# Storing the result of a decode kernel by four transfers on two queues instead of one on one queue

## The chip, the cores and the metric

The kernel runs on one core of a Trainium2 chip. The time is that of the device, in microseconds, for one execution of the program; beside it stands a profile of one such execution. A core has TensorE (PE; its weight loads are listed as PEld), VectorE (DVE), ScalarE (ACT), GpSimd (POOL) and SyncE (SP), and sixteen DMA engines that move data between HBM and the on-chip memory. In the profile a `q` behind an engine's name means its sequencer: the part that waits, branches and issues DMA transfers. L631 is line 631 of the kernel.

## The reference

Two blocks work on the same input x of 2 rows by 1024, and a gate mixes them. Block A is one decode step of attention with 32 query heads over 4 key and value heads and a cache of 32768 positions; block B is a mixer with a small MLP.

```
g = sigmoid((x * gate_w).sum(-1, keepdims=True))
q = (x @ wq), 32 heads of 128
p = softmax(q @ k.T * 128 ** -0.5)          # k_cache, v_cache: 2 x 4 x 32768 x 128
a = (p @ v) @ wo
h = gelu(layernorm(x) @ w1)                 # shifted along the sequence, which has length 1
x1 = x + shifted(h) @ w2
b = x1 + gelu(layernorm(x1) @ w3) @ w4
out = g * a + (1 - g) * b                   # 2 x 1 x 1024, float32
```

With a sequence of length 1 every shift moves h out of reach, so x1 is x, and w1 and w2 aren't read. What has to be read are the two caches and wq, w3, w4 and wo, 331 MB in float32; what is written are 8 KB.

## The kernel before

Everything is ordered by hand. Each engine has its own instruction stream, and a small class `Line` holds an engine and its semaphore: `after` makes the engine wait for marks of others, `mark` lets an instruction raise the engine's own semaphore, and `take` (L52) waits for a semaphore with a no-op and lowers it again.

All large loads are issued by SyncE through the helper `load` (L218), in the order of use, into two ring buffers `load0` and `load1` of 8 MB each: wq and w3 for the projections, then for each of eight pairs of batch row and key head two pieces of the keys (kt) and two of the values (vt), with w4 after the fourth pair, then wo. The end of wo goes into a buffer of its own, `tail`, by four transfers. The first two loads are issued ahead of everything (L246), and ScalarE issues one small load, that of x and the gate's weights (L279). Every load waits until TensorE has read what stood in its buffer.

TensorE, VectorE and ScalarE follow the loads in loops over the eight pairs. ScalarE's last work is its part of the copies in the eighth pair (L547). After the loop, TensorE multiplies the last rows of wo (`into_acc`, L372; `into_final`, L380), with the sum so far folded in by a product with a selection matrix (L617). VectorE copies one half of the final sums into `ahead` (L627) and adds the other half into `out_sb` (L630).

The result is laid out in 128 partitions of 64 numbers, of which every fourth partition holds a row that counts: 32 rows of 256 bytes. Partition 32g + 4r holds columns 64g to 64g + 63 of row r of `out`, which has 8 rows of 256 columns. One transfer stores them, issued by SyncE (L631). Behind it SyncE raises `issued` (L632), GpSimd waits for that and clears all semaphores but `stored` (L634), and ScalarE's `take` waits until the store has landed. That `take` is the last thing that the kernel does.

```
    dve.after(ended(2))
    sp.after(dve.mark(nc.vector.tensor_add(out_sb, final[1], ahead)))
    nc.sync.dma_start(out.rearrange("(q b) (g c) -> g (q b) c", q=G, g=G), out_sb[::SHIFT // B]).then_inc(stored, 16)
    nc.sync.nop().then_inc(issued, 1)
    nc.gpsimd.wait_ge(issued, 1)
    nc.clear_and_free_semaphores(cleared)
    act.take(stored, 16)
```

Here G is 4, CHUNK 64, SHIFT 8, B 2 and C 32.

Of the kernel before, what the change touches and what calls it, by code (L numbers as in the profile page):

```python
# [15 lines left out]
B, D, HQ, HKV, SK, DH, F = 2, 1024, 32, 4, 32768, 128, 3584  # L16
# [7 lines left out]
C = 32  # L24
G = P // C
# [3 lines left out]
SHIFT = C // G  # L29
CHUNK = D // G // G  # L30
# [42 lines left out]
def kernel(  # L73
# [52 lines left out]
    nc = tc.nc  # L126
    scale = DH ** -0.5

    def new(name, *shape, parts=P):
        return nc.alloc_sbuf_tensor(name, [parts, *shape], F32).ap()  # L130
# [51 lines left out]
    ahead = new("ahead", CHUNK)  # L182
    out_sb = new("out_sb", CHUNK)
# [5 lines left out]
    final = [sc[i][:, :CHUNK] for i in range(2)]  # L189
# [6 lines left out]
    def sem(name):  # L196
        cleared.append(nc.alloc_semaphore(name))
        return cleared[-1]

    stored = nc.alloc_semaphore("stored")  # L200
    pe, dve, act, pool = (Line(e, sem(n)) for e, n in (
        (nc.tensor, "pe"), (nc.vector, "dve"), (nc.scalar, "act"), (nc.gpsimd, "pool")))
    sp = Line(nc.sync)
# [4 lines left out]
    issued = sem("issued")  # L208
# [32 lines left out]
    def ended(i):  # L241
        return (pe.sem, SUMMED[1] + i)
# [32 lines left out]
    for mark, lo, hi in zip(came[1:], (0, 5, 7), (5, 7, 8)):  # L275
# [7 lines left out]
        out=ident, in_=ident, pattern=[[-1, P]], base=0, channel_multiplier=1,  # L283
# [343 lines left out]
    nc.vector.tensor_copy(ahead, final[0]).then_inc(own_step, 1)  # L627
    dve.take(own_step)
    dve.after(ended(2))
    sp.after(dve.mark(nc.vector.tensor_add(out_sb, final[1], ahead)))  # L630
    nc.sync.dma_start(out.rearrange("(q b) (g c) -> g (q b) c", q=G, g=G), out_sb[::SHIFT // B]).then_inc(stored, 16)  # L631
    nc.sync.nop().then_inc(issued, 1)  # L632
    nc.gpsimd.wait_ge(issued, 1)
    nc.clear_and_free_semaphores(cleared)  # L634
    act.take(stored, 16)


# ---- launch: one core; the host only lays the arrays out
# [28 lines left out]
```

## Time and profile before

| | |
|---|---|
| median of 3 runs | 773.53 us (773.42 to 773.77) |
| the profiled execution | 773.49 us |
| its span, first to last instruction | 772.0 us |
| read from HBM, written | 331.36 MB, 0.01 MB |
| mean rate over the span | 429 GB/s |
| TensorE, VectorE, ScalarE busy | 57%, 12%, 8% |

The span counts from the first instruction of any engine to the last; the time of the execution has 1.5 us more, which no row of the profile covers. Times in the views are in microseconds from the span's start, except durations in the rows by line, which are in nanoseconds (smallest, median and largest). A DMA row on a sequencer is the issue of a transfer, not its movement of data; that shows only in the share of the DMA engines, which the views by windows give for any stretch.

### The profile page before, as it was taken

The numbers are of one execution on the slowest core, as the hardware profiler recorded it, in microseconds if no ns is written. First come the engines' busy times: TensorE is split into PE (matmuls) and PEld (weight loads), VectorE is DVE, ScalarE is ACT, GpSimd is POOL, SyncE is SP. The second block draws the span as 40 slices with busy tenths as digits, with TensorE's granted clock in tenths as the row PEclk, the third lists the DMA queues.
The fourth block names the chain that finished last, engine by engine and source line by source line (L and its number), as shares of the span: only waits on it lengthen the run. The fifth ranks groups of instructions, "written<-read, shape, count | busy, mean of one in ns | idle before, by whom it ended". The sixth has DMA issues, their size and how long they took to land. (4 is left out here: it accounts for less than half of the span.)

```text
span 772.0 us, 7477 instructions
## 1 busy us (share of the span) xinstructions
PE 439.1 (57%) x3348; PEld 202.4 (26%) x3348; DVE 95.0 (12%) x274; ACT 60.4 (8%) x143; POOL 3.9 (1%) x14
## 2 busy tenths in 40 slices
PE   0676756464645474556475447454746564646466
PEld 0232413222322232223233213121323232313233
DVE  1110102100210021002100002100210021002110
ACT  0000002000200020002000002000200020002000
POOL 2000000000000000000000000000000000000000
PEclk9977668867787768767866677777776697678789
DMA  9999999999999999999999999999999999999997
GB/s 381 435 436 436 435 436 435 436 436 431 421 435 435 435 435 435 435 435 435 430 428 444 432 435 435 435 431 435 435 435 435 435 435 435 435 435 431 421 430 321
DMA packets 6668, 331.50 MB, mean 429 GB/s; under 512 B 900, under 2 KB 1028, under 8 KB 1284
## 3 DMA queue, kind: packets, MB, share of 16 engines
q1 hardware_dynamic: 6516, 331.36, 99.3%
q8 instruction: 7, 0.11, 0.1%
q10 hardware_dynamic: 144, 0.01, 0.0%
q14 instruction: 1, 0.01, 0.0%
HBM read 331.36 MB, written 0.01 MB: 429 GB/s over the span
## 5 line engine op out<-in xcount | busy, mean ns | idle before, releaser
L474 PE MATMUL sc<-load,q_cur 128*32 128x512 f32 x1024 | 149.4, 744 | 126.3 <-PEq L52 126.3
L500 PE MATMUL pv<-load,pt 128*32 128x512 f32 x1024 | 131.0, 670 | 92.5 <-PEq L52 92.5
L474 PEld LDWEIGHTS sc<-load,q_cur 128*32 128x32 f32 x1024 | 54.2, 133 | 215.4 <-issue 209.5
L500 PEld LDWEIGHTS pv<-load,pt 128*32 128x32 f32 x1024 | 39.4, 121 | 174.1 <-issue 174.1
L491 PE MATMUL sc<-wide,p 128*128 128x128 f32 x256 | 43.8, 344 | 22.8 <-PEq L52 22.8
L557 DVE TENSOR_REDUCE mx<-sc 128x1 f32<-128x512 f32 x32 | 21.4, 689 | 284.3 <-PE sc L474 284.3
L541 ACT ACT_TABLE_LOAD x8 | 10.3, 1283 | 490.5 <-ACTq L52 490.5
L491 PEld LDWEIGHTS sc<-wide,p 128*128 128x128 f32 x256 | 39.5, 182 | 30.0 <-issue 30.0
L372 PE MATMUL acc<-load,w_pad 128*32 128x256 f32 x448 | 33.9, 474 | 18.5 <-PEq L52 18.5
L574 DVE COPY pt<-sc 64x256 f32<-64x256 f32 x64 | 25.9, 415 | 73.4 <-PE sc L491 72.8
L547 ACT COPY pt<-sc 64x256 f32<-64x256 f32 x64 | 23.5, 368 | 77.4 <-PE sc L491 75.3
L579 DVE COPY pv_sb<-pv 128x512 f32<-128x512 f32 x16 | 10.3, 686 | 153.4 <-PE tr L506 153.4
L372 PEld LDWEIGHTS acc<-load,w_pad 128*32 128x32 f32 x448 | 18.6, 136 | 33.0 <-issue 28.2
L510 PE MATMUL tr<-sel,pv_sb 128*128 128x8 f32 x128 | 19.3, 287 | 11.8 <-PEq L52 11.8
L358 PE MATMUL sc<-load,x_pad 128*32 128x512 f32 x128 | 19.9, 790 | 3.8 <-PEq L52 3.8
L510 PEld LDWEIGHTS tr<-sel,pv_sb 128*128 128x128 f32 x128 | 18.8, 233 | 12.3 <-issue 12.3
L541 ACT ACTIVATE p<-sc,bias 128x512 f32<-128x512 f32 x32 | 21.6, 686 | 0.1
L358 PE MATMUL sc<-load,xn_pad 128*32 128x384 f32 (+1 forms) x128 | 16.0, 662 | 7.6 <-PEq L52 7.6
L343 PE MATMUL tr<-xg_sb,perm 128*128 128x16 f32 x4 | 1.0, 372 | 25.2 <-DMA xg_sb<-xg 25.2
L570 DVE COPY p<-p 128x256 f32<-128x256 f32 x32 | 9.4, 294 | 26.7 <-ACT p L541 26.7
L358 PEld LDWEIGHTS sc<-load,xn_pad 128*32 128x32 f32 x128 | 4.9, 133 | 18.7 <-issue 18.7
L358 PEld LDWEIGHTS sc<-load,x_pad 128*32 128x32 f32 x128 | 5.0, 138 | 17.8 <-issue 17.8
(93 smaller groups left out, 95.0 us busy)
## 6 DMA issues: line engine op xcount, KB each, us to landing
load<-w SPq DMA_DIRECT2D x4, 7168.0 KB, 24.5
load<-wo SPq DMA_DIRECT2D x1, 7168.0 KB, 29.0
load<-wo SPq DMA_DIRECT2D x1, 4608.0 KB, 18.9
load<-wo SPq DMA_DIRECT2D x1, 2560.0 KB, 24.7
tail<-wo SPq DMA_DIRECT2D x1, 1024.0 KB, 26.7
tail<-wo SPq DMA_DIRECT2D x1, 640.0 KB, 27.7
load<-kt SPq DMA_DIRECT2D x16, 29.7
load<-vt SPq DMA_DIRECT2D x16, 29.1
```

What stands on the lines that cost most here:

```text
L358: last = nc.tensor.matmul(b[C * g:C * g + C, :hi - lo], pad[:, k], t[:, o + lo:o + hi], start=(k == 0), stop=(k == KD - 1))
L372: inst = nc.tensor.matmul(acc[C * g:C * g + C], lhsT, rows[:, g * (D // G):(g + 1) * (D // G)], start=False, stop=last, skip_group_check=True)
L474: last = nc.tensor.matmul(sc[i][C * g:C * g + C], q_cur[:, w, s], ring[j][:, w, o:o + 512], start=(s == 0 and w == 0), stop=(s == 1 and w ...
L491: last = nc.tensor.transpose(sc[k][:, t * P:(t + 1) * P], pair.rearrange("p w q -> p (w q)"), ident)
L500: last = nc.tensor.matmul(pv[C * g:C * g + C], pt[j][w][:, lo:lo + C], ring[j][:, w, o:o + G * DH], start=(j == 0 and w == 0 and t == 0), ...
L510: last = nc.tensor.matmul(tr[1][:, w * REP:(w + 1) * REP], pv_sb[:, s, w].rearrange("p i q -> p (i q)"), sel[:, s], start=(s == 0), stop=( ...
L541: nc.scalar.activation(p[:, i, :, :PART], sc[i].rearrange("p (t q w) -> p t w q", t=NT, w=PART), AF.Exp, bias=bias, scale=scale, accum_out ...
L547: nc.scalar.copy(*halves(1, j, c)).then_inc(pt_in, 1)
L557: last = [nc.vector.reduce_max(out=mx[:, k:k + 1], in_=sc[k], axis=AX.X) for k in ((1, 2) if i == 2 else (i,))][-1]
L570: nc.vector.tensor_copy(p[:, i, :, PART], p[:, i, :, 0]).then_inc(to_pe, 1)
L574: nc.vector.tensor_copy(*halves(0, j, c)).then_inc(pt_in, 1)
L579: last = nc.vector.tensor_copy(pv_sb[:, :, :, i], pv.rearrange("p (s q w) -> p s w q", q=HALF, w=PART))
```

## The change

The transfer with three dimensions (four blocks of columns, eight rows, 64 numbers) becomes four transfers with two dimensions, one for each block of columns. SyncE issues the first and the third, ScalarE the second and the fourth. Both engines wait for the same addition, both raise `issued` when they are done, GpSimd waits for two instead of one, and ScalarE's `take` waits for the landing of all four.

```
-    sp.after(dve.mark(nc.vector.tensor_add(out_sb, final[1], ahead)))
-    nc.sync.dma_start(out.rearrange("(q b) (g c) -> g (q b) c", q=G, g=G), out_sb[::SHIFT // B]).then_inc(stored, 16)
-    nc.sync.nop().then_inc(issued, 1)
-    nc.gpsimd.wait_ge(issued, 1)
+    added = dve.mark(nc.vector.tensor_add(out_sb, final[1], ahead))
+    for line in (sp, act):
+        line.after(added)
+    for g in range(G):
+        line = (sp, act)[g % 2]
+        line.e.dma_start(out[:, g * CHUNK:(g + 1) * CHUNK], out_sb[C * g:C * g + C:SHIFT // B]).then_inc(stored, 16)
+    for line in (sp, act):
+        line.e.nop().then_inc(issued, 1)
+    nc.gpsimd.wait_ge(issued, 2)
     nc.clear_and_free_semaphores(cleared)
-    act.take(stored, 16)
+    act.take(stored, 16 * G)
```

## The prediction

> **What bounds the kernel now.** I read the page's head and its DMA lines first, to see what the 772 us are spent on.
>
> ```profile
> span 772.0 us, 7477 instructions
> ...
> DMA  9999999999999999999999999999999999999997
> ...
> q1 hardware_dynamic: 6516, 331.36, 99.3%
> ```
>
> The sixteen DMA engines are full from the first slice to the last but one, so the kernel as a whole is a stream of weights and caches from HBM. The change touches none of that: it edits the store of the result, which is issued once the stream has ended. A stage of two microseconds is in question, and the limit of that stage is a chain, not a bandwidth. So the second view is the chain that ended last, from its last piece of the stream on.
>
> ```profile
> 740.75 27.75 DMA tail<-wo
> 768.49 0.04 issue
> 768.53 0.77 PE sc L380 x40
> 769.30 0.11 PE sc L617 x8
> 769.41 0.46 PE sc L380 x24
> 769.87 0.02 issue
> 769.89 0.23 DVE out_sb L630
> ```
>
> The last load lands at 768.49, TensorE and VectorE finish the last products, and the addition into out_sb ends at 769.89 + 0.23 = 770.12. The chain view stops at this instruction of an engine, though the span goes on to 772.0. What follows stands in the rows by line: the issue on SyncE (L631), the mark behind it (L632), GpSimd's clearing of semaphores (L634), and the one instruction of ScalarE that waits for the store (L52, the helper `take`).
>
> ```profile
> SPq L631 <- DVE out_sb L630: 28.0, 1, 28.0
> ...
> L631 SPq DMA_DIRECT2D out<-out_sb x1: 672/672/672, 770.1 to 770.1; - x1
> ...
> L632 SPq EVENT_SEMAPHORE  x1: 17/17/17, 770.9 to 770.9; - x1
> ...
> L634 POOLq DRAIN  x1: 82/82/82, 770.9 to 770.9; - x1
> L634 POOLq EVENT_SEMAPHORE_RANGE_CLEAR  x1: 135/135/135, 771.0 to 771.0; - x1
> ...
> L52 ACTq EVENT_SEMAPHORE  x1: 17/17/17, 771.9 to 771.9; - x1
> ```
>
> The third view is the busy time by windows, cut where the DMA engines begin and end their work for the store.
>
> ```profile
> 770.15:770.82 0.67, 0.00 (x0) 0.00 (x0) 0.00 (x0) 0.00 (x0) 0.00 (x0) 1.00 0.00 0
> 770.82:771.42 0.60, 0.00 (x0) 0.00 (x0) 0.00 (x0) 0.00 (x0) 0.00 (x0) 1.00 0.00 0
> 771.42:771.60 0.18, 0.00 (x0) 0.00 (x0) 0.00 (x0) 0.00 (x0) 0.00 (x0) 0.94 0.20 44
> 771.60:771.96 0.36, 0.00 (x0) 0.00 (x0) 0.00 (x0) 0.00 (x0) 0.00 (x0) 0.50 0.00 0
> ```
>
> The second last number of a row is the mean share of the sixteen DMA engines, the last one GB/s. So the tail reads: 0.03 from the addition to the issue, 0.67 of issue, 0.60 in which the issue is over and no packet runs, 0.18 of packets, and 0.35 until ScalarE's `take` at about 771.95, just ahead of the end of the span. Together 1.83 us, 0.24% of the run. Nothing covers any of it: no engine is busy in these rows. The measured execution is 773.49, that is 1.5 beyond the span; that part lies behind ScalarE's last instruction and I let it move with it.
>
> **The change part by part.** It removes one issue of 0.67 on SyncE. It adds two issues on SyncE and two on ScalarE, each of 8 rows of 256 bytes, a wait of ScalarE for the addition, a second mark, and a count of two for GpSimd. The bytes stay the same (32 rows, 8 KB). Only the terms 0.67 and 0.18 can change in kind; the 0.60 and the 0.35 are latencies that the last of four transfers pays as the one transfer did, so I keep them at the rows.
>
> The price of an issue with two dimensions is not in the trace for a store, but it is for loads:
>
> ```profile
> L218 SPq DMA_DIRECT2D load<-kt x16: 327/328/328, 70.0 to 663.2; - x16
> ...
> L218 SPq DMA_DIRECT2D tail<-wo x4: 432/432/432, 740.3 to 741.7; - x4
> ...
> L246 SPq DMA_DIRECT2D load<-wq x2: 387/400/412, 0.7 to 1.2; - x2
> ...
> L279 ACTq DMA_DIRECT2D xg_sb<-xg x1: 372/372/372, 2.4 to 2.4; - x1
> ...
> 740.27 1.85 SPq L218 DMA_DIRECT2D tail<-wo  x4
> ```
>
> The issues of kt come alone, behind a wait, and take 0.328. The four of tail come right behind another issue and take 0.432 each; four of them fill 1.85, so the three gaps are (1.85 − 4 × 0.432) / 3 = 0.04. ScalarE's only issue, of xg, took 0.372. So two issues on one queue at the loads' price take 0.328 + 0.04 + 0.432 = 0.80, and on ScalarE 0.372 + 0.04 + 0.432 = 0.84. That is already more than the single 0.67: even if the third dimension was the whole reason for the dearer store, what is bought back on the first issue is spent on the second. The other bound is the store's own row: 0.672 + 0.04 + 0.672 = 1.38 for two, and 1.49 if the second also pays the 0.104 by which 0.432 exceeds 0.328. The new transfers share the two dimensions with the loads, and the direction, the short rows and the few partitions with the store. I take the side of the loads, since dimensions are what an issuing sequencer has to work through, but only two thirds of the way: 0.80 + (1.38 − 0.80) / 3 = 0.99. The last issue then ends 0.99 − 0.67 = 0.32 later than now. The bounds are +0.13 and +0.82; a bound below nothing needs an issue cheaper than any in the trace, and stands as a rival.
>
> Both queues start together, since ScalarE waits for the same mark as SyncE. Nothing is queued behind ScalarE's new wait but its own two issues, its mark and the final `take`. ScalarE's last work before that ended long ago:
>
> ```profile
> 718.97 1.68 ACT L547 COPY pt<-sc 64x256 f32<-64x256 f32 x4 [8.38 <-PE sc L491]
> ```
>
> That is some 49 us ahead of the issue, so no activation stands in front of the new issues. The two marks are 0.017 each (L632) and lie behind the issues on their queues, where only GpSimd waits for them. GpSimd's drain and clear end at 771.0 + 0.135, about 0.34 behind the end of the issue, while `take` comes 1.13 behind it (771.95 − 770.82). Both move with the last issue, so the clear keeps some 0.8 us of cover and costs nothing; without that cover it would cost its own 0.2.
>
> The packets: 0.20 of sixteen engines for 0.18 us is a mean of 3.2 engines at work, so the one transfer runs on few engines, with several rows behind each other on each. Four transfers of 8 rows that start apart have less to do behind the last issue, a quarter of the rows: between no gain and 0.18 × 3/4 = 0.13 less. I take 0.06 less, about the middle of the two.
>
> The Trainium skill (DMA: Bandwidth & Descriptors, section Rules for kernel authors) speaks against the change: it says to coalesce small transfers, because under 64 KB one pays mostly overhead. The windows agree, with 0.18 us of packets in a tail of 1.83; by that rule alone, with nothing gained on the packets, the sum would be +0.32 in place of the sum below.
>
> The sum: +0.32 for the issues, −0.06 for the packets, +0.26 in all. Against the profiled execution that is 773.49 + 0.26 = 773.75; the median of the runs shown is 0.04 higher, 773.53, and gives 773.79, so 773.8. With the bounds the forecast runs from +0.13 − 0.13 = 0 to +0.82, that is from 773.5 to 774.35.
>
> **The rivals.**
>
> *The two queues take turns at the loads' price.* If the issues of SyncE and ScalarE pass through one shared part, splitting them over two engines buys nothing, and the four stand in line. For it speaks the difference of 0.104 between a lone load and one that follows another: something of the one before is still occupied. Against it: the trace has no two issues at the same time on the two queues, and 128 rows may occupy the shared part for longer than 8. The time: 0.328 + 3 × (0.432 + 0.04) = 1.74 until the last issue ends, 1.07 more than now, less 0.06: +1.01, or 774.5. The Trainium skill (Perfetto Trace Analysis, section DMA Instruction — HWDGE (DVE, Sync)) states such a rule: the block that generates descriptors is shared and is locked for one issue at a time, and the wait for the lock is part of the profiled duration. No row of this trace shows it across two queues.
>
> *The two queues take turns at the store's price: slower.* The same place, but the occupied part is the whole issue and the price is that of L631, because short rows to HBM and not the third dimension make it dear. Then the four take 4 × 0.672 + 3 × 0.04 = 2.81, 2.14 more than now, less 0.06: +2.08, or 775.6. It decides from the point where the last issue ends 1.55 + 0.06 = 1.61 later than now, that is where the four in line take over 2.28, some 0.54 each beside the gaps. For it: the only store of the trace costs twice a lone load. Against it: both conditions must hold together.
>
> *Issues of few rows are cheap.* If the price goes with the rows, an issue of 8 costs far less than one of 128. At half of 0.328 two take 0.16 + 0.04 + 0.16 = 0.36, 0.31 less than now, and with the packets at their lower bound −0.44: 773.1. Against it: the store's 32 rows cost more than the loads' 128, and kt with its long rows costs no more than xg with its short ones, so rows aren't what is paid for. Even this is no more than 0.06%: the whole tail of 1.83 would have to go nearly to nothing for a gain over 0.2%.
>
> *The change doesn't do what it says.* If the third dimension isn't what costs, each transfer keeps 0.67 on queues that are independent: 1.38, so +0.71 − 0.06 = +0.65, 774.2. This lies in the forecast's bounds and has no chance of its own.
>
> **How the numbers follow.** Forecast, independent queues with prices between the loads' and the store's: 0.58. Turns at the loads' price: 0.20. Turns at the store's price: 0.11. Cheap issues: 0.07. The rest, 0.04, is for something outside the tail, half of it to each side. A measurement of this kernel can tell about 0.2% from no change, here 1.55 us, so below 772.0 is faster and above 775.1 slower. Faster is only half of the rest, 0.02; slower is the rival at the store's price and the other half, 0.13; within is 0.85. The runs shown differ by 0.35 among themselves. The range has to hold the forecast (0.58), the turns at the loads' price (0.20) and a little of the cheap issues, so I set it from 773.3 to 774.9; outside are the turns at the store's price, most of the cheap issues and the rest, not quite 2 in 10.
>
> **What would show it.** In the rows by line, two issues of out on SyncE and two on ScalarE, all from about 770.15, the first between 0.33 and 0.67 and the second the same or 0.1 longer; the last ends near 771.1. Forecast right: SyncE's and ScalarE's issues overlap in time and no first issue is longer because of the other queue. Turns: ScalarE's first issue shows about twice SyncE's duration. In the windows, packets begin about 0.6 behind an issue, in two or more separate groups, and `take` comes about 0.35 behind the last packet. The forecast is wrong if the last issue ends by 770.8 or after 772.4, if the stretch between the last packet and `take` grows with four transfers, or if `take` isn't the last instruction any more.

## The result, and the profile after

The changed kernel takes 774.92 us in the median (774.60 to 775.27, 20 runs) against 773.50 for the kernel before on the same chips (773.28 to 773.77, 20 runs). The ratio is 1.0018, with a 95% interval from 1.0011 to 1.0025: 1.42 us slower. The profiled execution took 774.88, with a span of 773.4.

The stream of loads hasn't moved. The page's DMA lines and the timeline at the end of the kernel after:

```profile
DMA  9999999999999999999999999999999999999996
...
q1 hardware_dynamic: 6512, 331.36, 99.2%
```

```profile
769.90 0.23 DVE L630 TENSOR_TENSOR out_sb<-sc,ahead 128x64 f32<-128x64 f32 x1 [0.15 <-PE sc L380]
770.15 1.46 SPq L635 DMA_DIRECT2D out<-out_sb  x2
770.15 2.14 ACTq L635 DMA_DIRECT2D out<-out_sb  x2
```

The addition ends at 770.13 as it did before (770.12), and both queues start their issues at 770.15. So in these two profiles the whole loss lies behind this point. (That q1, SyncE's queue, has 6512 packets in place of 6516 is the store's doing: its part of them fell from 36 to 32.) The rows by line of the four issues (now L635, smallest, median and largest duration in ns), of the two marks and of ScalarE's `take`:

```profile
L635 SPq DMA_DIRECT2D out<-out_sb x2: 641/704/767, 770.2 to 771.0; - x2
L635 ACTq DMA_DIRECT2D out<-out_sb x2: 642/1055/1468, 770.2 to 771.7; - x2
...
L637 SPq EVENT_SEMAPHORE  x1: 17/17/17, 771.7 to 771.7; - x1
L637 ACTq EVENT_SEMAPHORE  x1: 17/17/17, 772.3 to 772.3; - x1
...
L52 ACTq EVENT_SEMAPHORE  x1: 17/17/17, 773.4 to 773.4; - x1
```

SyncE's pair fills 1.46, so its two issues are 0.77 and 0.64 with a gap of 0.05. ScalarE's pair fills 2.14: one issue of 1.47, one of 0.64, a gap of 0.03. The busy time by windows, cut where packets run (the second last number is the share of the sixteen DMA engines):

```profile
770.15:771.51 1.36, 0.00 (x0) 0.00 (x0) 0.00 (x0) 0.00 (x0) 0.00 (x0) 1.00 0.00 0
771.51:771.60 0.09, 0.00 (x0) 0.00 (x0) 0.00 (x0) 0.00 (x0) 0.00 (x0) 1.00 0.13 23
771.60:771.78 0.18, 0.00 (x0) 0.00 (x0) 0.00 (x0) 0.00 (x0) 0.00 (x0) 1.00 0.00 0
771.78:771.87 0.09, 0.00 (x0) 0.00 (x0) 0.00 (x0) 0.00 (x0) 0.00 (x0) 1.00 0.13 23
771.87:772.25 0.38, 0.00 (x0) 0.00 (x0) 0.00 (x0) 0.00 (x0) 0.00 (x0) 1.00 0.00 0
772.25:772.34 0.09, 0.00 (x0) 0.00 (x0) 0.00 (x0) 0.00 (x0) 0.00 (x0) 1.00 0.14 23
772.34:772.94 0.60, 0.00 (x0) 0.00 (x0) 0.00 (x0) 0.00 (x0) 0.00 (x0) 1.00 0.00 0
772.94:773.03 0.09, 0.00 (x0) 0.00 (x0) 0.00 (x0) 0.00 (x0) 0.00 (x0) 1.00 0.13 23
773.03:773.37 0.34, 0.00 (x0) 0.00 (x0) 0.00 (x0) 0.00 (x0) 0.00 (x0) 1.00 0.00 0
```

There are four short bursts, one for each transfer, and the DMA view of each names its queue: SyncE's, ScalarE's, SyncE's, ScalarE's. The last one ends the kernel. Its issue starts at 770.15 + 1.47 + 0.03 = 771.65, which is 1.50 later than the only issue of before. From there to its packets pass 772.94 − 771.65 = 1.29 (before 771.42 − 770.15 = 1.27), the packets last 0.09 (before 0.18), and from the last packet to `take` pass 0.34 (before 0.35). So 1.50 + 0.02 − 0.09 − 0.01 = 1.42. What made ScalarE's first issue 1.47 long, and what would have decided without it, is what the experiments are about. The times of before given with them are those of the same chips.

### The profile page after: what moved, and what is told of

Its sections match the earlier page's. It is cut to its first block, busy times and chain, and to the rows that moved or that the text cites. A ratio compares the mean times of both kernels' runs of the same rounds, so it can differ in the third digit from the quotient of the medians.

```text
span 773.4 us, 7481 instructions
## 1 busy us (share of the span) xinstructions
PE 443.2 (57%) x3348; PEld 202.9 (26%) x3348; DVE 96.0 (12%) x274; ACT 60.4 (8%) x143; POOL 3.7 (0%) x14
## 3 DMA queue, kind: packets, MB, share of 16 engines
q1 hardware_dynamic: 6512, 331.36, 99.2%
## 5 line engine op out<-in xcount | busy, mean ns | idle before, releaser
L474 PE MATMUL sc<-load,q_cur 128*32 128x512 f32 x1024 | 151.9, 756 | 124.6 <-PEq L52 124.6
L474 PEld LDWEIGHTS sc<-load,q_cur 128*32 128x32 f32 x1024 | 51.4, 135 | 219.0 <-issue 214.8
L510 PE MATMUL tr<-sel,pv_sb 128*128 128x8 f32 x128 | 21.5, 305 | 11.8 <-PEq L52 11.8
L510 PEld LDWEIGHTS tr<-sel,pv_sb 128*128 128x128 f32 x128 | 21.0, 257 | 12.3 <-issue 12.3
```

Source lines behind the costliest of these rows:

```text
L474: last = nc.tensor.matmul(sc[i][C * g:C * g + C], q_cur[:, w, s], ring[j][:, w, o:o + 512], start=(s == 0 and w == 0), stop=(s == 1 and w ...
L510: last = nc.tensor.matmul(tr[1][:, w * REP:(w + 1) * REP], pv_sb[:, s, w].rearrange("p i q -> p (i q)"), sel[:, s], start=(s == 0), stop=( ...
```

## The experiments

**All four transfers on one queue.** The edit of the first puts every issue on SyncE, the second puts every issue on ScalarE.

```
-        line = (sp, act)[g % 2]
-        line.e.dma_start(out[:, g * CHUNK:(g + 1) * CHUNK], ...)
+        sp.e.dma_start(out[:, g * CHUNK:(g + 1) * CHUNK], ...)     # second kernel: act.e
```

> All four transfers of 8 rows are issued by SyncE, none by ScalarE. Theory of turns (the two queues pass their issues through one shared part, and a store of 8 rows costs 0.64 us of it whatever queue it comes from): no issue is longer than 0.67, the four take about 4 x 0.64 + 3 x 0.05 = 2.7, and the time is about 775.5. If SyncE pays 0.77 for the first even with no issue of ScalarE beside it, the 0.13 over 0.64 is the price of a first issue and not of the other queue. Rival (ScalarE's first issue is slow by itself, 1.47, because it has issued nothing for 768 us; nothing is shared): SyncE's four again take 2.7, 775.5. This run alone doesn't tell them apart; it gives the price of an issue without company.

> All four transfers of 8 rows are issued by ScalarE, none by SyncE. Turns: ScalarE's first issue falls from 1.47 to at most 0.77, since SyncE isn't in the way; the four take about 2.7, and the time is about 775.5, as with all four on SyncE. Rival (ScalarE's first issue is slow by itself): the first stays at 1.47, the four take 1.47 + 3 x 0.64 + 3 x 0.05 = 3.5, and the time is about 776.4.

Measured: 775.62 on SyncE (before 773.51, ratio 1.0027, 1.0017 to 1.0037), 776.00 on ScalarE (same kernel before, ratio 1.0032, 1.0020 to 1.0044). The row of the issues, first of SyncE's kernel, then of ScalarE's:

```profile
L633 SPq DMA_DIRECT2D out<-out_sb x4: 626/633/766, 770.2 to 772.3; - x4
```

```profile
L633 ACTq DMA_DIRECT2D out<-out_sb x4: 646/648/1225, 770.1 to 772.7; - x4
```

Each engine pays a surcharge on its first issue with no other queue beside it: SyncE 0.766 against 0.63, ScalarE 1.225 against 0.648. So the theory of turns, as it was put here, is wrong for most of what makes ScalarE's 1.47 longer than 0.65, and the rival right for that part: 0.58 is ScalarE's own. Neither is all of it; 1.468 − 1.225 = 0.24 only appears beside SyncE.

**An early store on ScalarE, or SyncE a little later.** Two kernels let ScalarE issue a store of constants some 50 us ahead, once with 8 rows and once with 32; a third delays SyncE.

```
+    nc.scalar.dma_start(out[G * B:, :CHUNK], wide[:C:SHIFT // B, :CHUNK]).then_inc(warmed, 16)   # 8 rows
+    act.take(warmed, 16)                                     # second kernel: wide[::SHIFT // B, :CHUNK], 32 rows
     added = dve.mark(nc.vector.tensor_add(out_sb, final[1], ahead))
```

```
-    for line in (sp, act):
-        line.after(added)
+    act.after(added)
+    sp.after(dve.mark(nc.vector.tensor_copy(so_far[:, :CHUNK], final[0])))
```

> The changed kernel, and ScalarE issues one more store of 8 constant rows of 256 bytes (to HBM behind the result, where the host drops it) as soon as its loop is done, some 50 us before the result. Theory A (an engine pays a surcharge on its first store; ScalarE's is 0.58, 1.23 against 0.65): the surcharge falls to the early store, the first store of the result costs 0.65, or up to 0.24 more if the company of SyncE's issues costs that by itself; the last issue ends 1.36 to 1.6 behind the first one's start in place of 2.14, and the time is 774.2 to 774.4. Theory B (turns of the two queues make it long): ScalarE's first stays at 1.4 and the time at 774.9.

> The changed kernel with an early store on ScalarE as before, but of 32 rows, which is spread over all sixteen DMA engines. If the surcharge belongs to an engine's first store of any shape, it is gone from the result's first issue (0.65) and the time is 774.6. If it belongs to the first transfer over fewer than sixteen engines, ScalarE's first issue of 8 rows is still 1.2 to 1.5 and the time 774.9.

> The changed kernel, but SyncE waits for one more short copy of VectorE behind the addition (into a buffer that nothing reads any more), so that its first issue starts about 0.1 behind ScalarE's. Theory (in the changed kernel ScalarE's first issue pays its own surcharge, 1.23, and 0.24 for the turn that SyncE has ahead of it): ScalarE now has the first turn, its first issue takes 1.18 to 1.25, its second starts 0.24 earlier, and the time is 774.6 to 774.7 although SyncE starts later. Rival (1.47 is what ScalarE pays beside SyncE in any order): the time stays at 774.9 or is above it.

Measured: 774.60 with the early 8 rows (before 773.48, ratio 1.0014, 1.0005 to 1.0023), 774.62 with the early 32 rows (before 773.52, ratio 1.0014, 1.0005 to 1.0023), 774.80 with SyncE later (before 773.55, ratio 1.0016, 1.0007 to 1.0025). The rows of the issues in the first of them, the early one and those of the result:

```profile
L631 ACTq DMA_DIRECT2D out<-wide x1: 1227/1227/1227, 720.8 to 720.8; - x1
...
L638 SPq DMA_DIRECT2D out<-out_sb x2: 707/740/774, 770.3 to 771.1; - x2
L638 ACTq DMA_DIRECT2D out<-out_sb x2: 648/652/655, 770.3 to 771.0; - x2
```

```profile
770.28 1.33 ACTq L638 DMA_DIRECT2D out<-out_sb  x2
770.28 1.53 SPq L638 DMA_DIRECT2D out<-out_sb  x2
```

The surcharge went with the early store (1.227), and ScalarE's issues of the result cost 0.65 each. By the timeline all four issues are over at 770.28 + 1.53 = 771.81, where the changed kernel has 770.15 + 2.14 = 772.29. And yet the time is still 1.12 above that of before, and not the 774.2 to 774.4 that theory A expected. The windows of the same kernel show why:

```profile
770.28:771.58 1.30, 0.00 (x0) 0.00 (x0) 0.00 (x0) 0.00 (x0) 0.00 (x0) 1.00 0.00 0
771.58:771.67 0.09, 0.00 (x0) 0.00 (x0) 0.00 (x0) 0.00 (x0) 0.00 (x0) 1.00 0.13 23
771.67:771.94 0.27, 0.00 (x0) 0.00 (x0) 0.00 (x0) 0.00 (x0) 0.00 (x0) 1.00 0.00 0
771.94:772.03 0.09, 0.00 (x0) 0.00 (x0) 0.00 (x0) 0.00 (x0) 0.00 (x0) 1.00 0.13 23
772.03:772.30 0.27, 0.00 (x0) 0.00 (x0) 0.00 (x0) 0.00 (x0) 0.00 (x0) 1.00 0.00 0
772.30:772.39 0.09, 0.00 (x0) 0.00 (x0) 0.00 (x0) 0.00 (x0) 0.00 (x0) 1.00 0.13 23
772.39:772.66 0.27, 0.00 (x0) 0.00 (x0) 0.00 (x0) 0.00 (x0) 0.00 (x0) 1.00 0.00 0
772.66:772.76 0.10, 0.00 (x0) 0.00 (x0) 0.00 (x0) 0.00 (x0) 0.00 (x0) 1.00 0.13 21
```

The bursts begin exactly 0.36 apart (771.58, 771.94, 772.30, 772.66), from the two queues in turns, though both queues started together, and between the bursts no packet runs. The four transfers of both queues stand in one line behind the issues, and three turns of 0.36 are 1.08. Not all of that is waiting: SyncE's second issue starts at 770.28 + 0.77 + 0.05 = 771.10, 0.82 behind its first, whatever ScalarE does. Its packets run at 772.66, 1.56 later in place of 1.27 to 1.29, and of this the issue's own row shows only 0.07 (0.707 against 0.64). SyncE's first transfer waits as long, 771.94 − 770.28 = 1.66 in place of the changed kernel's 1.36, and its issue shows nothing of it (0.774 against 0.767).

The early 32 rows do not take the surcharge away: ScalarE's first issue of the result is still 1.182.

```profile
L631 ACTq DMA_DIRECT2D out<-wide x1: 574/574/574, 722.0 to 722.0; - x1
...
L638 ACTq DMA_DIRECT2D out<-out_sb x2: 653/918/1182, 770.1 to 771.3; - x2
```

So the surcharge belongs to the first transfer of 8 rows, not to the first store, and an idle queue isn't the reason either. That answers the issue's part as expected; the time does not fit the expectation, 774.62 and not 774.9, because the DMA view gives the first burst of this kernel to ScalarE's queue: its first issue had the first turn and was spared the 0.24. That is what the third kernel tests. With SyncE 0.13 later (770.19 against 770.06), ScalarE's first issue took 1.224, as long as without company, although SyncE's queue was just as busy:

```profile
L635 ACTq DMA_DIRECT2D out<-out_sb x2: 646/935/1224, 770.1 to 771.3; - x2
L635 SPq DMA_DIRECT2D out<-out_sb x2: 640/703/766, 770.2 to 771.0; - x2
```

```profile
770.06 1.90 ACTq L635 DMA_DIRECT2D out<-out_sb  x2
770.19 1.46 SPq L635 DMA_DIRECT2D out<-out_sb  x2
```

So the 0.24 comes with SyncE's transfer ahead and goes when ScalarE's is the first; I read it as the wait for SyncE's turn. The last packets of this kernel show nearly the same gain:

```profile
772.65:772.75 0.10, 0.00 (x0) 0.00 (x0) 0.00 (x0) 0.00 (x0) 0.00 (x0) 1.00 0.12 21
```

They begin 772.65 − 770.06 = 2.59 behind the first issue, in the changed kernel 772.94 − 770.15 = 2.79. The time itself can't show it: the median is 0.12 under that of the changed kernel, less than the 0.2 to 0.3 expected, the two weren't run side by side, and the intervals of their ratios overlap.

**What makes an issue dear.** Four kernels store by one transfer of SyncE, into an output of 32 rows of 64; what they change is the shape or the count.

```
-    for g in range(G): ...                        # the four transfers
+    nc.sync.dma_start(out, out_sb[::SHIFT // B]).then_inc(stored, 16)                  # 32 rows
+    nc.sync.dma_start(out[:, :2], out_sb[::SHIFT // B]).then_inc(stored, 16)           # 16 x 2 rows, apart in HBM
+    nc.sync.dma_start(out[:24], out_sb[:96:SHIFT // B]).then_inc(stored, 16)           # 24 rows
+    nc.sync.dma_start(out, out_sb[::SHIFT // B]).then_inc(stored, 32)                  # 32 rows, counted with 32
```

> One transfer from SyncE with two dimensions, 32 rows of 256 bytes, into an output that lies in HBM as 32 rows of 64 (the host reorders them, as it did before). Theory that the first dimension sets the price (4 rows or blocks, or 8, are spread over few DMA engines, 32 over all sixteen): the issue costs what a lone load costs, 0.33, the packets take less, and the time is 773.5 - 0.34 - 0.1 = 773.05. Rival (a store to HBM of short rows is dear whatever its shape): the issue stays at 0.64 to 0.67 and the time is 773.4.

> One transfer from SyncE with three dimensions on the side of HBM, 16 x 2 x 64, where the 16 blocks lie apart (an output of 16 x 3 x 64, of which a third isn't written; the host leaves it out). Theory that the first dimension sets the price: 0.33, as with two dimensions, 773.05. Theory that three dimensions cost: 0.67 here and 0.33 with 32 rows in two dimensions, 773.4. If both this and the two-dimensional one stay at 0.64 or more, it is the store itself.

> One transfer with two dimensions of 24 rows from SyncE, which leaves out the last 8 of the 32 rows of the result. With 24 rows the work isn't spread over all sixteen DMA engines. If the spread over fewer engines costs at the issue (8 rows: 0.766 as SyncE's first, 32 rows: 0.537), the issue is 0.75 and the time 773.7; if it is the number of rows, between the two and near 0.6.

> One transfer with two dimensions of 32 rows, whose landing is counted with 32 in place of 16, so that the sequencer has to add a part of the count itself though all sixteen DMA engines work. If that part of the count is the dear one: 0.75 to 0.77 for the issue in place of 0.537, and 773.7. If it costs nothing: 0.54 and 773.45.

Measured: 773.46, 773.54, 773.67 and 773.40; before 773.51, 773.51, 773.48 and 773.48, and all four intervals include 1. The times can't tell these kernels apart, but the issues can. In the order of the edits, one kernel a fence:

```profile
L632 SPq DMA_DIRECT2D out<-out_sb x1: 537/537/537, 770.2 to 770.2; - x1
```

```profile
L632 SPq DMA_DIRECT2D out<-out_sb x1: 631/631/631, 770.2 to 770.2; - x1
```

```profile
L632 SPq DMA_DIRECT2D out<-out_sb x1: 891/891/891, 770.0 to 770.0; - x1
```

```profile
L632 SPq DMA_DIRECT2D out<-out_sb x1: 585/585/585, 770.0 to 770.0; - x1
```

The third dimension costs 0.09 (0.631 against 0.537), the larger count 0.05. The count's 0.585 lies between the two prices that were expected for it. 24 rows cost 0.891, more than 32 and more than 8 (0.766), and more than the 0.75 expected, so it isn't the number of rows alone. The DMA view of the stretch of the packets counts them by queue, here with 32 rows, with 24, for the first burst of the changed kernel with 8, and last for the store of the kernel before:

```profile
q1 hardware_dynamic: 48, 0.01, 7.0%
```

```profile
q1 hardware_dynamic: 36, 0.01, 7.7%
```

```profile
q1 hardware_dynamic: 16, 0.00, 10.0%
```

```profile
q1 hardware_dynamic: 36, 0.01, 7.5%
```

Beyond one packet for each row that leaves 16, 12, 8 and 4. The Trainium skill (DMA: Bandwidth & Descriptors, section Why a DMA increments its semaphore by 16 and not by 1) says that each engine that takes part posts one completion, and that their number is the largest up to 16 that divides the outer dimension of both sides; these counts agree, so I read them as 16, 12, 8 and 4 engines. Fewer than sixteen engines is what the dear ones of 8 and 24 rows have in common, but it isn't the whole price: the store of before, by four engines and with three dimensions, takes 0.672, only 0.04 more than the 0.631 of sixteen engines with three dimensions. From 8 to 12 engines the price rises, and the number of rows for each engine changes along with it; these runs don't separate the two. Both theories on the 32 rows missed the issue: 0.54 is neither a load's 0.33 nor the 0.64 of 8 rows.

**One transfer of 8 rows, two of 16, and one of 32 with an early store.** The first is the changed kernel's first transfer by itself; the second uses both queues at once with all sixteen engines; the third puts a store of constants of the same shape behind the last load on SyncE.

```
+    nc.sync.dma_start(out[:8], out_sb[:32:SHIFT // B]).then_inc(stored, 16)            # one of 8 rows
+    line.e.dma_start(out[16 * i:16 * i + 16], out_sb[64 * i:64 * i + 64:SHIFT // B])   # two of 16, i = 0 on SyncE, 1 on ScalarE
+    nc.sync.dma_start(out[G * G * B:], wide[::SHIFT // B, :CHUNK])                     # ahead of the one of 32
```

> One transfer of 8 rows from SyncE, which leaves out the other 24 rows of the result: the first of the changed kernel's four by itself. Theory (the loss comes from the number of transfers, which take turns at 0.36, and from ScalarE's surcharge): the issue is 0.77 as in the changed kernel, its packets begin 1.36 behind the issue and last 0.08 in place of 0.18, and the time is that of the kernel before, 773.5. Rival (a transfer of 8 rows is itself slower to land): over 773.8.

> Two transfers with two dimensions and 16 rows each, one from SyncE and one from ScalarE at the same time, into an output of 32 rows of 64. Theory A (a surcharge on an engine's first store): SyncE 0.54 as with its 32 rows, ScalarE 0.54 plus a surcharge as before, up to 1.1; its packets still begin 1.2 to 1.4 behind its start, so the time is 773.5 to 773.7. Theory B (turns): ScalarE's packets begin 0.3 to 0.5 behind SyncE's, 773.8 to 774.0. If ScalarE's issue is no longer than SyncE's, the surcharge belongs to transfers of 8 rows, not to first stores.

> One transfer with two dimensions and 32 rows, and ahead of it, behind the last load, SyncE issues a store of the same shape of 32 constant rows (to HBM behind the result, where the host drops it). If an engine pays a surcharge on its first transfer of a kind, the result's issue falls from 0.54 to between 0.33 and 0.43, and the time to 773.25 to 773.4, the least of all the kernels. If stores of short rows cost 0.54 each time, it stays at 773.45.

Measured: 773.52 for the one of 8 rows (before 773.52), with 0.766 for its issue, both as its theory expected: one such transfer costs as much time as the one of 32 rows with three dimensions. The two of 16 rows take 773.70 (before 773.48; ratio 1.0004, 0.9995 to 1.0013). Their issues, and the windows of the same kernel:

```profile
L634 SPq DMA_DIRECT2D out<-out_sb x1: 552/552/552, 770.3 to 770.3; - x1
L634 ACTq DMA_DIRECT2D out<-out_sb x1: 573/573/573, 770.3 to 770.3; - x1
```

```profile
771.50:771.67 0.17, 0.00 (x0) 0.00 (x0) 0.00 (x0) 0.00 (x0) 0.00 (x0) 1.00 0.14 24
771.67:771.77 0.10, 0.00 (x0) 0.00 (x0) 0.00 (x0) 0.00 (x0) 0.00 (x0) 1.00 0.00 0
771.77:771.95 0.18, 0.00 (x0) 0.00 (x0) 0.00 (x0) 0.00 (x0) 0.00 (x0) 1.00 0.14 23
```

ScalarE's first store over sixteen engines costs hardly more than SyncE's (0.573 against 0.552), and the bursts still come one behind the other, 0.27 apart. The time is the one of its theory A, the order of the bursts that of theory B. 0.27 isn't a matter of the 16 rows: the first two bursts of the changed kernel, of 8 rows each, are as far apart (771.51 and 771.78). The one of 32 rows with an early store:

```profile
L635 SPq DMA_DIRECT2D out<-out_sb x1: 473/473/473, 770.0 to 770.0; - x1
```

Its issue takes 0.473 where the early one paid 0.537, between the two values that were expected. The time is 773.35 (before 773.52), the least of all; its ratio of 0.9997 has an interval from 0.9988 to 1.0006, so that it beats the kernel before isn't shown.

## Why the prediction was right or wrong

**Right: where, and within what.** The loss lies in the tail behind the addition and nowhere else; it is 0.18%, within the 0.2% that the forecast gave the most chance; GpSimd's clear stayed covered (it starts at 772.5, `take` at 773.4); the latency to `take` behind the last packet stayed (0.34 against 0.35), and the packets gave back about what the sum said (0.09 against 0.06). But the median of 774.92 is 1.1 above the forecast of 773.8 and a hair above the range's 774.9. That it comes so near the range's end is luck: the range reached that far for turns at 0.47 behind one another, and what filled it is for the larger part a surcharge that no rival had. The sign that the forecast is wrong, a last issue that ends after 772.4, didn't show either (772.29), though the forecast's mechanism was.

**Wrong: the price of an issue.** The step was to place two issues two thirds of the way from the store's row to the loads', because two dimensions are what they share with the loads. The reason given, that dimensions are what an issuing sequencer works through, isn't borne out: the third dimension is worth 0.09 of 0.63. The other things that they share with the store decide, and of these the runs vary only the number of rows and, with it, of engines: an issue of 8 rows costs 0.64, near the store's price. SyncE's pair took 1.46, near the 1.38 of the other bound, which is +0.71 and not +0.32. The rival "the change doesn't do what it says" had this price right for SyncE, though not the independent queues, and was given no chance of its own.

**Missing: ScalarE's surcharge.** The prediction took ScalarE for SyncE's equal on the strength of one row, 0.372 for the load of x. That load goes to sixteen engines (144 packets on q10, ScalarE's queue, for 128 rows). The first issue of 8 rows costs 0.58 more on ScalarE. How much of that the time loses, the medians can't tell: the kernel with the early 8 rows takes 774.60, and the one with the early 32 rows, which keeps the surcharge and was spared only the 0.24, 774.62. In the profiles the last packets begin 2.79 behind the first issue in the changed kernel, 772.58 − 770.06 = 2.52 with the early 32 rows and 772.66 − 770.28 = 2.38 with the early 8. So of the 0.58 only 0.14 is won beyond the turn; SyncE's own two issues and the turns fill the rest.

**Half right: the turns.** The forecast had the queues independent, and they aren't. The rival of turns at the loads' price, with 0.47 for a turn, gave 774.5, and the kernel that has no surcharge takes 774.60 with turns of 0.36; that the two times agree is chance. Its place was wrong: the turns show in the packets, not as longer issues, except for the 0.24 that ScalarE's first issue waits. The sign that the prediction named for turns, a first issue of ScalarE about twice as long as SyncE's, was there (1.468 against 0.767), and 0.58 of it had nothing to do with turns. The forecast kept the 0.60 between issue and packets, which is no constant: behind ScalarE's 1.225 with no company it is 771.50 − 770.12 − 1.225 = 0.16. From the start of a later issue of 8 rows to its packets pass 1.27 to 1.29 when nobody is ahead, and 1.56 for the last in line; for an engine's first one it is 1.36 to 1.38, and for the 32 rows 1.17. The rule in the Trainium skill (Perfetto Trace Analysis, section DMA Instruction — HWDGE (DVE, Sync)), that one shared block makes the descriptors for one issue at a time, fits bursts that come one behind another, 0.27 or 0.36 apart; that the wait for it lies in the issue's profiled duration fits the 0.24 but only 0.07 of the 0.29 of SyncE's second and none of the 0.30 of its first.

**The sum as measured.** The last issue starts 1.50 later: 0.65 for ScalarE's first as any issue of 8 rows, 0.58 surcharge, 0.24 for SyncE's turn, 0.03 gap. Without the surcharge SyncE's second transfer is the last: its issue starts 0.82 later, its packets wait 0.29 longer, and 0.09 comes off for the packets, about +1.0.

**Open.** What the surcharge is made of, why ScalarE's is 0.58 and SyncE's 0.13, whether it belongs to 8 rows, to 8 engines or to any number under sixteen (of the transfers under sixteen, only those of 8 rows were repeated on a queue), and for how long an early store keeps it away beyond the 50 us tried here. Why a store over sixteen engines still costs more at the issue (0.47 to 0.57) than a load (0.33 to 0.43). What sets the distance of the bursts at 0.27 or 0.36, and why a wait shows in ScalarE's issue and not in SyncE's.

## What to carry to other kernels

The last store of a kernel is a chain of latencies, 1.83 us here with 0.18 of data in it, so splitting it into four added to it, and there was little to win. One transfer with two dimensions over all sixteen engines had the cheapest issue (0.54 against 0.67), and laying the output out in HBM in the order of the partitions gives that without further work on the chip; that it saves time isn't shown here (773.46 against 773.51). Before work moves to another queue, look whether that queue has issued such a transfer before: one row of another shape is not a price.

## What the runs showed of the hardware that was not expected

- An engine's first transfer of 8 rows, over eight DMA engines, costs more at the issue than its later ones: 0.13 on SyncE (0.766 against 0.63), 0.58 on ScalarE (1.225 against 0.648). On ScalarE an earlier store over sixteen engines doesn't take it away (1.182), an earlier one over eight does (0.655).
- The surcharge hardly delays the packets of its own transfer; it holds up the next issue. With all four on ScalarE the first packets come 1.38 behind the start of an issue that takes 1.225 (1.29 behind one that takes 0.64), and the second ones 1.16 behind the first:

```profile
770.12:771.50 1.38, 0.00 (x0) 0.00 (x0) 0.00 (x0) 0.00 (x0) 0.00 (x0) 1.00 0.00 0
771.50:771.59 0.09, 0.00 (x0) 0.00 (x0) 0.00 (x0) 0.00 (x0) 0.00 (x0) 1.00 0.13 23
771.59:772.66 1.07, 0.00 (x0) 0.00 (x0) 0.00 (x0) 0.00 (x0) 0.00 (x0) 1.00 0.00 0
```

- Transfers of two queues reach the DMA engines one after the other while their issues overlap: 0.36 apart in the kernel with the early 8 rows, 0.27 apart with 16 rows each and for the first two of the changed kernel.
